# The first two w_in steps in four pieces each, and a room that the list now knows of

## The chip, the cores and the metric

The kernel runs on one core of a Trainium2 chip. The metric is the device time of one execution in microseconds; of the kernel before, three runs gave a median of 867.49 (867.4 to 868.03). Engines are named as in the profile: PE is TensorE (matmuls; PEld its weight loads), DVE is VectorE, ACT is ScalarE, POOL is GpSimd, SP is SyncE, which here issues DMAs.

## The reference

Attention inside chunks of 64 positions, and then a feed-forward layer whose nonlinearity is h·cos(h), all in fp32:

```python
scores = scale * np.matmul(q_c, k_c.transpose(0, 1, 2, 4, 3))
scores = scores - np.max(scores, axis=-1, keepdims=True)
attn = np.exp(scores)
attn = attn / (np.sum(attn, axis=-1, keepdims=True) + 1e-09)
out = np.matmul(attn, v_c)
...
x = np.ascontiguousarray(attn_out.transpose(0, 2, 1, 3)).reshape(B * S, H * D)
...
h = x @ w_in
g = h * np.cos(h)
return (g @ w_out).astype(np.float32)
```

q, k and v are (8, 8, 576, 64): 4608 tokens, 8 heads of 64. w_in is 512 x 2048, w_out 2048 x 512.

## The kernel before

**Tiles and steps.** The tokens are nine tiles of 512 (index t). The 512 columns of x are four groups of 128, one for each pair of heads (hp, or cc in the hidden layer); the 2048 hidden columns are 16 blocks of 128 (fc). A step is one tile with one block. `hidden` makes the block's h for the tile: each operand is split into a high and a low part, and each of the four groups of x takes three matmuls (high·high, high·low, low·high), twelve in all, which add up in one PSUM bank named h. There are two such banks. `activated` turns h into g = h·cos(h) in six pieces that alternate between ACT and DVE: a rounding (ACT, L497), the range reduction (DVE, L498), the sine (ACT, L499), the product with h (DVE, L500, the last reader of the bank h), g's high part (ACT, L501) and its low part (DVE, L502). `project` multiplies g by a block of w_out, twelve matmuls into the four banks acc, three steps behind `hidden` (LAG).

**Order of the steps.** Tile 0 with blocks 0 to 7 (steps 0 to 7), tile 1 with all 16 (steps 8 to 23), tile 0 with blocks 8 to 15 (steps 24 to 31), then tiles 2 to 8. While the first 32 steps run, the weights arrive over DMA and are split: a joining on DVE (L255, after two ACT pieces), a high part (ACT, L270) and a remainder (DVE, L275).

**Attention.** For tiles 0 and 1 `early` works by pairs of heads: scores on PE, a maximum (L333) and a subtraction (L337) on DVE, the exponential on ACT (L376), sums (L386) and a reciprocal on DVE, the quotient (L396, on POOL for tile 1 and for pairs 0 and 1 of tile 0, on DVE for the others), transposes on PE (L405), a copy on ACT (L411), and the weighted sum on PE. Then x goes into two parts: a cast on ACT (L460) and a remainder on DVE (L463). For tile 2 `attend_third` does the same for two groups of two pairs, with transposes on DVE (L422). The banks a0 and a1 carry the scores and the weighted sums of tiles 1 and 2, each in turn, so a later use waits for the last reader of the earlier one.

**x's room.** Tiles 0 and 1 have rooms of their own; tile 2's x is written into tile 1's (`x_room`). It can be written when step 23, the last of tile 1, has read what stood there.

**What sets the order.** Up to step 31 every piece of work on PE, ACT, DVE, POOL and SP is entered in a list with `piece(engine, length, run, *after, lag=...)`: its length in us as the list takes it, and the pieces that it comes after. `in_order` tries 1500 variations of due times, places each on the list's own clock (`placed`), keeps the best and gives the order in which all instructions are issued. Each engine then runs its instructions strictly in that order, and waits at the head of its queue for what the data need, whether the list knew of the need or not. The list before did not have an edge from step 23 to the casts of tile 2's x. From step 32 on a loop with an order written by hand takes over, which the change does not touch.

Of the kernel before, what the change touches and what calls it, by code (L numbers as in the profile page):

```python
# [11 lines left out]
F32 = mybir.dt.float32  # L12
# [9 lines left out]
P = 128  # L22
TOK = 512
# [8 lines left out]
GROUP = 8  # L32

EARLY = 2

PAIRED = 9

# [121 lines left out]
def attention_then_cos_ffn(ctx: ExitStack, tc, qT, kT, v, w_in, w_out, out, wide):  # L159
# [147 lines left out]
    def bank(kind, i):  # L307
        if kind == "a":
            b = ps_a.tile([P, 512], F32, name=f"a{i % 2}")
        else:  # L310
            b = ps_o.tile([P, 512], F32, name=f"acc{i}")
        return b
# [160 lines left out]

    partial = [hbm.tile([P, DM], F32, name=f"partial{sub}") for sub in range(NSUB)]

    def hidden(t, fc):
        h = ps_h.tile([P, TOK], F32, name="h")
        w_hi, w_lo = w_parts["in", fc]
        for cc in range(NCC):
            x_hi, x_lo = (x[:, cc % 2] for x in x_parts[t, cc // 2])  # L480
            ws = slice(cc * P, (cc + 1) * P)
            matmul(h, w_hi[:, ws], x_hi, start=(cc == 0), stop=False)
            matmul(h, w_hi[:, ws], x_lo, start=False, stop=False)
            matmul(h, w_lo[:, ws], x_hi, start=False, stop=(cc == NCC - 1))
        return h
# [119 lines left out]
    def piece(eng, length, run, *after, at=0.0, lag=0.15, port=False, table=None):  # L605
        port = port or eng == POOL
        work.append([eng, length, run, [a for a in after if a is not None], at, length + lag, port, table])
        return len(work) - 1
# [28 lines left out]
    def made_by(key, run, *args):  # L637

        def go():
            made[key] = run(*args)  # L640
        return go

    def rest_of(key, i):
        return lambda: made[key][i]()
# [26 lines left out]
    def early(t):  # L671
        s, e, z, q, w, p = {}, {}, {}, {}, {}, {}
        for hp in range(HP):
            which = ("a", hp % 2) if t else ("acc", hp)
            key = ("s", t, hp)
            s[hp] = piece(
                PE, 1.0, made_by(key, lambda hp=hp, which=which: scores_early(t, hp, bank(*which))),
                banks_free.get(("a", hp % 2)) if t else None,
                at=here["qk", t, hp], lag=0.35,
            )  # L680
            m = piece(DVE, 0.6, rest_of(key, 0), s[hp])
            room = turned_out.get((t - 1, hp // 2))
            banks_free[which] = piece(DVE, 0.6, rest_of(key, 1), m, room)
            e[hp] = piece(ACT, 0.6, lambda hp=hp: exponentials(t, hp), banks_free[which], table=AF.Exp)
# [9 lines left out]
        for hp in range(HP):  # L694
            key = ("t", t, hp)
            at = banks_free["a", hp % 2] if t else p.get(hp - 2)
            turned_out[t, hp // 2] = turned = piece(
                PE, 0.6, made_by(key, transposed, t, hp), q[hp], at, w.get(hp - 2), lag=0.35
            )
            p[hp] = piece(ACT, 0.5, lambda key=key: made[key](), turned, w.get(hp - 2))  # L700
            if t:
# [4 lines left out]
            if t and hp % 2 == 0:  # L706
# [3 lines left out]
            n = len(hps)  # L710
            key = ("x", t, hp)
            now = piece(
                PE, 0.9 * n, made_by(key, lambda hps=hps, which=which: weighted(t, hps, [bank(*b) for b in which])),
                *(p[j] for j in hps), *(banks_free.get(b) for b in which),
                at=here["v", 0, hp] if t == 0 else 0.0, lag=0.35,
            )
# [13 lines left out]
    ahead = early(1)  # L730


    def attend_third(begin):
        t = 2
        below = []
        for g in range(2):
# [16 lines left out]
        for g in range(2):  # L753
# [17 lines left out]
                        load_v(t, hp)  # L771
                piece(SP, 0.1, values_next, w)
            for i in (0, 2):
                hi = piece(ACT, 0.45, rest_of(key, i), w)
                banks_free["a", i // 2] = piece(DVE, 0.6, rest_of(key, i + 1), hi)
                x_done.setdefault(t, []).append(banks_free["a", i // 2])

# [17 lines left out]
    for s in range(STAGE):  # L795
        t, fc = order[s]
        key = ("h", s)
        bank_at = held.get(s - 2) if s > 1 else None
        stream = piece(
            PE, 2.72, made_by(key, hidden, t, fc), stream, split["in", fc], bank_at,  # L800
            *x_done[t], *([turned_out[0, 1]] if s < 2 else ()),
        )
        hid = stream
        if s == GROUP:
            def prefetch_third():
# [35 lines left out]
                held[s] = a  # L841
        given[s] = a
        if s == GROUP + 7:
            attend_third(hid)

    for i in in_order(work, x_done[2]):
        work[i][2]()
# [70 lines left out]
```

## Time and profile before

| what | us |
|---|---|
| median of three runs | 867.49 (867.4 to 868.03) |
| the profiled execution | 865.84 |
| its span, first to last instruction | 864.1 |

The profile is of one execution. A row of its timeline has a start, a duration, the engine, the line, the operation with its tiles, the count of instructions merged into it, and, in brackets, the idle time of the engine just before and what ended it. The rows that carry the argument stand in the prediction.

### The profile page before, as it was taken

The page shows a single profiled execution, that of the slowest core. Times are in us where ns is not written, and L with a number is a line of the kernel's source. Part 1 is how long each engine was busy: PE and PEld are TensorE (multiplying, and loading weights), DVE is VectorE, ACT ScalarE, POOL GpSimd, SP SyncE. Part 2 cuts the span into 40 slices and gives each one's busy share as a digit, 9 for nine tenths or more (in the row PEclk, how much of TensorE's full clock was granted, in tenths as well). Part 3 has the DMA queues.
Part 4 walks back from the last instruction along what each step waited for, and adds up shares of the span by engine and source line. Part 5 has one row for each costly group of instructions (what it writes and reads, how often), then busy time and mean ns, then how long its engine had stood idle before and what let it go on. Part 6 is the DMA issues. An engine that isn't in the chain of part 4 may idle for free.

```text
span 864.1 us, 14053 instructions
## 1 busy us (share of the span) xinstructions
PE 845.4 (98%) x5792; PEld 695.1 (80%) x5792; DVE 555.0 (64%) x942; ACT 389.5 (45%) x636; POOL 7.5 (1%) x12
## 2 busy tenths in 40 slices
PE   6999999799999999999999999999999999999998
PEld 5778888688888888888888888888888888888886
DVE  6979878644686567665776468645865577644332
ACT  5999963333433335333533353334433353333332
POOL 1020000000000000000000000000000000000000
PEclk9999999999999999999999999999999999999999
DMA  9990200320103000300130010301030010001001
GB/s 344 416 376 34 75 2 26 120 99 2 50 1 122 25 13 37 123 25 2 49 110 15 25 49 15 109 25 50 1 122 25 2 50 25 1 1 49 1 1 49
DMA packets 26559, 57.52 MB, mean 67 GB/s; under 512 B 2944, under 2 KB 2944, under 8 KB 26496
## 3 DMA queue, kind: packets, MB, share of 16 engines
q1 hardware_dynamic: 26496, 56.63, 18.1%
q8 instruction: 45, 0.74, 0.4%
q14 instruction: 18, 0.15, 0.0%
HBM read 46.14 MB, written 10.49 MB: 66 GB/s over the span
## 4 chain that ended last, share of the span: by engine, by line
PE 92%; DVE 1%; issue 0%; ACT 0%
PE acc L193 45%; PE h L193 43%; PE a L193 4%; DVE pts L422 1%; DVE x L463 0%; DVE g L498 0%; PE a L405 0%; DVE x L561 0%; ACT x L460 0%; DVE g L500 0%
## 5 line engine op out<-in xcount | busy, mean ns | idle before, releaser
L193 PE MATMUL h<-x,w_in 128*128 128x512 f32 x1728 | 417.2, 390 | 4.8 <-DVE g L500 4.8
L193 PEld LDWEIGHTS h<-x,w_in 128*128 128x128 f32 x1728 | 324.9, 188 | 72.8 <-DVE g L500 5.3
L193 PE MATMUL acc<-w_out,g_hi 128*128 128x512 f32 x1152 | 358.4, 392 | 0.0
L193 PEld LDWEIGHTS acc<-w_out,g_hi 128*128 128x128 f32 x1152 | 214.0, 188 | 45.5 <-ACT pts L559 0.3
L193 PE MATMUL acc<-w_out,g_lo 128*128 128x512 f32 x576 | 224.4, 390 | 0.0
L498 DVE SCALAR_TENSOR_TENSOR g<-g,h 128x512 f32<-128x512 int32 x144 | 98.6, 685 | 143.4 <-ACT g L497 142.5
L497 ACT ACTIVATE g<-h 128x512 int32<-128x512 f32 x144 | 85.8, 596 | 195.2 <-PE h L193 194.8
L502 DVE TENSOR_TENSOR g_lo<-g,g_hi 128x512 fp32r<-128x512 f32 x144 | 99.6, 691 | 75.3 <-ACT g_hi L501 73.1
L499 ACT ACTIVATE g<-g 128x512 f32<-128x512 f32 x144 | 91.2, 633 | 124.5 <-DVE g L498 124.4
L501 ACT CAST g_hi<-g 128x512 fp32r<-128x512 f32 x144 | 89.4, 621 | 124.6 <-DVE g L500 78.2
L500 DVE TENSOR_TENSOR g<-h,g 128x512 f32<-128x512 f32 x144 | 99.5, 691 | 53.7 <-ACT g L499 50.6
L193 PEld LDWEIGHTS acc<-w_out,g_lo 128*128 128x128 f32 x576 | 108.1, 188 | 22.8
L422 DVE STREAM_TRANSPOSE pts<-e 32x256 f32<-32x256 f32 x224 | 97.4, 435 | 3.7
L463 DVE TENSOR_TENSOR x<-a,x 128x512 fp32r<-128x512 f32 (+1 forms) x36 | 22.3, 654 | 7.7 <-ACT x L460 7.7
L386 DVE TENSOR_REDUCE z<-e 128x8 f32<-128x512 f32 x36 | 23.7, 678 | 3.2 <-ACT e L376 3.2
L255 DVE SCALAR_TENSOR_TENSOR w<-w,half 128x512 uint32<-128x512 uint32 x32 | 22.6, 713 | 2.8 <-ACT half L262 1.6
L193 PEld LDWEIGHTS a<-kt,qt 64*64 64x64 f32 x1024 | 18.3, 135 | 7.4 <-issue 5.6
L376 ACT ACTIVATE e<-e 128x1024 f32<-128x1024 f32 (+1 forms) x22 | 19.1, 900 | 9.2 <-DVE e L337 9.1
L193 PE MATMUL a<-kt,qt 64*64 64x64 f32 x1024 | 20.6, 221 | 1.6 <-DVE x L463 1.6
L193 PEld LDWEIGHTS a<-pts,vt 64*64 64x64 f32 x1056 | 17.3, 137 | 6.0 <-issue 4.6
L460 ACT CAST x<-a 128x512 fp32r<-128x512 f32 (+1 forms) x36 | 18.5, 565 | 7.7 <-PE h L193 7.2
L396 DVE TENSOR_TENSOR e<-e,z 128x512 f32<-128x512 f32 x30 | 20.3, 683 | 0.0
(50 smaller groups left out, 252.2 us busy)
## 6 DMA issues: line engine op xcount, KB each, us to landing
qt<-in_qT_dram SPq DMA_DIRECT2D x36, 256.0 KB, 4.9
kt<-in_kT_dram SPq DMA_DIRECT2D x36, 256.0 KB, 5.1
vt<-in_v_dram SPq DMA_DIRECT2D x34, 256.0 KB, 3.7
w_in<-in_w_in_dram SPq DMA_DIRECT2D x16, 512.0 KB, 9.7
w_out<-in_w_out_dram SPq DMA_DIRECT2D x16, 512.0 KB, 9.9
out_dram<-w SPq DMA_DIRECT2D x16, 256.0 KB, 2.2
out_dram<-half SPq DMA_DIRECT2D x16, 256.0 KB, 2.1
out_dram<-x SPq DMA_DIRECT2D x4, 256.0 KB, 2.0
```

The costliest lines, as they stand in the source:

```text
L193: kept(nc.tensor.matmul(*args, **kw))
L255: kept(nc.vector.scalar_tensor_tensor(bits, bits, 3, low, op0=ALU.logical_shift_left, op1=ALU.bitwise_or))
L386: kept(nc.vector.tensor_reduce(out=sums_of(t)[:, hp], in_=weights_of(t, hp // 2)[:, hp % 2], op=ALU.add, axis=AX.X))
L396: kept(eng.tensor_tensor(e, e, zb, op=ALU.mult))
L422: kept(nc.vector.transpose(out=dst[o : o + BL, :, qb], in_=src[i : i + BL, :, kb]))
L463: kept(nc.vector.tensor_tensor(lo, xq, hi.bitcast(F32), op=ALU.subtract))
L497: lambda: kept(nc.scalar.activation(n, h, AF.Identity, bias=0.25, scale=0.5 / math.pi)),
L498: lambda: kept(nc.vector.scalar_tensor_tensor(g, n, -2.0 * math.pi, h, op0=turns, op1=over)),
L499: lambda: kept(nc.scalar.activation(g, g, AF.Sin, bias=0.5 * math.pi)),
L500: lambda: kept(nc.vector.tensor_tensor(g, h, g, op=ALU.mult)),
L501: lambda: kept(nc.scalar.copy(out=g_hi, in_=g)),
L502: lambda: kept(nc.vector.tensor_tensor(g_lo, g, g_hi.bitcast(F32), op=ALU.subtract)),
```

## The change

The edits:

- `hidden` can do a part of the four groups of x, and go on in a bank that it began.
- Steps 0 and 1 (`s < APART`) enter the list as four pieces of three matmuls each, one per pair of heads. Each comes after its own pair's x only, where a whole block came after all four.
- The casts of tile 2's x come after `room`, which is the hidden block of step 23. For this the list gets `attend_third` eight steps later in the program text (at `GROUP + NFC - 1`), with the same `begin`.
- Three lengths in the list are shorter: scores 0.95 for 1.0, transposes 0.53 for 0.6, weighted sums 0.55 a pair for 0.9.
- No matmul, no DMA and no piece of ACT or DVE work is added or taken away, except that tables for ACT's functions are loaded where the order asks for them.

```diff
-    def hidden(t, fc):
-        h = ps_h.tile([P, TOK], F32, name="h")
+    def hidden(t, fc, ccs=range(NCC), h=None):
+        if h is None:
+            h = ps_h.tile([P, TOK], F32, name="h")
         w_hi, w_lo = w_parts["in", fc]
-        for cc in range(NCC):
+        for cc in ccs:
...
-                PE, 1.0, made_by(key, lambda hp=hp, which=which: scores_early(t, hp, bank(*which))),
+                PE, 0.95, made_by(key, lambda hp=hp, which=which: scores_early(t, hp, bank(*which))),
...
-                hi = piece(ACT, 0.45, rest_of(key, i), w)
+                hi = piece(ACT, 0.45, rest_of(key, i), w, room)
...
-        stream = piece(
-            PE, 2.72, made_by(key, hidden, t, fc), stream, split["in", fc], bank_at,
-            *x_done[t], *([turned_out[0, 1]] if s < 2 else ()),
-        )
+        if s < APART:
+            for cc in range(NCC):
+                run = lambda key=key, t=t, fc=fc, cc=cc: made.update(
+                    {key: hidden(t, fc, (cc,), made.get(key))})
+                stream = piece(
+                    PE, 0.68, run, stream, split["in", fc], bank_at, turned_out[0, 1],
+                    *x_done[t][2 * cc : 2 * cc + 2], lag=0.15 if cc == NCC - 1 else 0.0,
+                )
+        else:
+            stream = piece(
+                PE, 2.72, made_by(key, hidden, t, fc), stream, split["in", fc], bank_at, *x_done[t],
+            )
...
-            attend_third(hid)
+            begin = hid
+        if s == GROUP + NFC - 1:
+            attend_third(begin, hid)
```

The list makes a new order of all that comes before step 32. The lines of the kernel move with the diff: L193 becomes L195, L460 L462, L463 L465, L497 L501, L498 L502, L499 L503, L500 L504. The order below step 32 is the same.

On PE, at the first hidden step. Before, the last weighted sum of tile 0 (a1_407, a0_406) is followed by two score groups of tile 1 (a0_438, a1_458), and then step 0 (h_479) with x of pairs 0 and 1 (x0_333, x0_334) and of pairs 2 and 3 (x0_400, x0_401):

```order
L193 MATMUL a1_407<-pts_372,x1_148 64x64 x2
L193 MATMUL a0_438<-kt_153,qt_152 64x64 x16
L193 MATMUL a1_458<-kt_157,qt_156 64x64 x16
L193 MATMUL h_479<-x0_333,w_in0_357 128x512
L193 MATMUL h_479<-x0_334,w_in0_357 128x512
...
L193 MATMUL h_479<-x0_400,w_in0_357 128x512
L193 MATMUL h_479<-x0_401,w_in0_357 128x512
```

and now, where step 0 is h_428, pairs 0 and 1 are x0_334 and x0_335, and pairs 2 and 3 x0_403 and x0_404:

```order
L195 MATMUL acc3_409<-pts_372,x1_148 64x64 x2
L195 MATMUL h_428<-x0_334,w_in0_369 128x512
L195 MATMUL h_428<-x0_335,w_in0_369 128x512
...
L195 MATMUL a1_442<-kt_157,qt_156 64x64 x16
L195 MATMUL a0_465<-kt_153,qt_152 64x64 x16
L195 MATMUL h_428<-x0_403,w_in0_369 128x512
L195 MATMUL h_428<-x0_404,w_in0_369 128x512
```

The first six matmuls of step 0 moved ahead of the two score groups; the other six stand behind them. Step 1 is cut in the same way around the third score group, where it stood whole between the third and the fourth. On DVE, ahead of this, the second pair's sum and the first reciprocal of tile 0 moved behind the third pair's subtraction and the fourth pair's maximum, and the join of w_in 0 moved behind the quotients of pairs 2 and 3.

On ACT, where tile 2's first x is cast. Before, h_1679, h_1757 and h_1804 are steps 21, 22 and 23, and x1_1753 is the high part of x:

```order
L499 ACTIVATE g_1710<-g_1710 128x512
L501 CAST g_hi_1711<-g_1710 128x512
L460 CAST x1_1753<-a0_1719 128x8x64
L460 CAST x1_1753<-a1_1720 128x8x64
L497 ACTIVATE g_1795<-h_1757 128x512
L497 ACTIVATE g_1834<-h_1804 128x512
L499 ACTIVATE g_1795<-g_1795 128x512
L499 ACTIVATE g_1834<-g_1834 128x512
```

and now, with h_1756 and h_1802 for steps 22 and 23:

```order
L503 ACTIVATE g_1710<-g_1710 128x512
L505 CAST g_hi_1711<-g_1710 128x512
L501 ACTIVATE g_1793<-h_1756 128x512
L503 ACTIVATE g_1793<-g_1793 128x512
L505 CAST g_hi_1794<-g_1793 128x512
L501 ACTIVATE g_1834<-h_1802 128x512
L462 CAST x1_1753<-a1_1720 128x8x64
L462 CAST x1_1753<-a0_1719 128x8x64
L503 ACTIVATE g_1834<-g_1834 128x512
```

Both casts moved behind all of step 22 and the first piece of step 23. On DVE the remainders that belong to them moved likewise, and on PE the second weighted sum of tile 2 moved from ahead of a projection to behind it.

On ACT again, some 25 instructions after the first sine: before, g_696 is step 4, and e0 and e1 are the exponentials of tile 1:

```order
L497 ACTIVATE g_696<-h_658 128x512
L260 ACTIVATE w_701<-w_out3_98 128x512
L376 ACT_TABLE_LOAD
L376 ACTIVATE e0_455<-e0_455 128x512
L499 ACT_TABLE_LOAD
L499 ACTIVATE g_696<-g_696 128x512
L376 ACT_TABLE_LOAD
L376 ACTIVATE e1_521<-e1_521 128x512
```

and now, with g_722 for step 4:

```order
L378 ACT_TABLE_LOAD
L378 ACTIVATE e0_459<-e0_459 128x512
...
L378 ACTIVATE e1_531<-e1_531 128x512
L262 ACTIVATE w_719<-w_out3_98 128x512
L501 ACTIVATE g_722<-h_654 128x512
L378 ACTIVATE e1_531<-e1_531 128x512
L272 CAST w_in6_741<-w_691 128x512
L503 ACT_TABLE_LOAD
L503 ACTIVATE g_722<-g_722 128x512
```

The sine of step 4 moved behind all three exponentials that were spread over three loads of their table; between the first sine and the last of these exponentials there were four table loads after the first sine's, and now there are two.

More of the change, by code (lines that the diff above doesn't have):

```diff
@@ L34 @@
 EARLY = 2
+APART = 2
 PAIRED = 9
@@ L697, in early @@
             turned_out[t, hp // 2] = turned = piece(
-                PE, 0.6, made_by(key, transposed, t, hp), q[hp], at, w.get(hp - 2), lag=0.35
+                PE, 0.53, made_by(key, transposed, t, hp), q[hp], at, w.get(hp - 2), lag=0.35
             )
@@ L712, in early @@
             now = piece(
-                PE, 0.9 * n, made_by(key, lambda hps=hps, which=which: weighted(t, hps, [bank(*b) for b in which])),
+                PE, 0.55 * n, made_by(key, lambda hps=hps, which=which: weighted(t, hps, [bank(*b) for b in which])),
                 *(p[j] for j in hps), *(banks_free.get(b) for b in which),
@@ L730, in attention_then_cos_ffn, with attend_third @@
     ahead = early(1)
-    def attend_third(begin):
+    def attend_third(begin, room):
         t = 2
```

## The prediction

> **What bounds the kernel now.** I read the page's first and fourth parts, then the busy times stretch by stretch, then TensorE's own waits.
>
> ```profile
> span 864.1 us, 14053 instructions
> PE 845.4 (98%) x5792; PEld 695.1 (80%) x5792; DVE 555.0 (64%) x942; ACT 389.5 (45%) x636; POOL 7.5 (1%) x12
> PE 92%; DVE 1%; issue 0%; ACT 0%
> ```
>
> TensorE (PE) is busy for 845.4 of 864.1 us and holds 92% of the chain that ended last. The change removes no matmul, so it can only win idle TensorE time and the time in which TensorE runs below full clock. The busy times by stretch (PE, PEld, DVE, ACT, POOL, granted clock, DMA) say where those lie:
>
> ```profile
> 0.00:25.00 25.00, 15.39 (x337) 13.75 (x337) 16.45 (x33) 13.49 (x27) 2.74 (x8) 0.93 0.95 353
> 25.00:60.00 35.00, 35.00 (x269) 28.28 (x268) 29.76 (x50) 33.92 (x56) 4.77 (x4) 1.00 1.01 408
> 60.00:100.00 40.00, 39.34 (x235) 32.20 (x235) 35.42 (x58) 39.52 (x75) 0.00 (x0) 1.00 0.28 95
> 100.00:140.00 40.00, 40.00 (x294) 32.86 (x293) 34.96 (x60) 25.82 (x42) 0.00 (x0) 1.00 0.00 1
> 140.00:180.00 40.00, 35.16 (x265) 28.33 (x265) 24.89 (x46) 12.62 (x22) 0.00 (x0) 0.96 0.24 79
> 330.00:864.00 534.00, 530.50 (x3388) 436.37 (x3386) 324.17 (x551) 203.91 (x325) 0.00 (x0) 1.00 0.11 37
> ```
>
> Idle are 9.61 us before 25, 0.66 between 60 and 100, 4.84 between 140 and 180, and 3.50 in the last stretch (the program's end, which the change does not touch). ACT, 45% busy over the span, is full from 25 to 100: 33.92 of 35 and 39.52 of 40. There a delay on ACT finds little slack to hide in.
>
> **Term A, the third tile's x.** TensorE around the 4.84 (start, duration, instruction), and below it the same kinds of work undisturbed:
>
> ```profile
> 157.02 0.61 PE L193 MATMUL acc<-w_out,g_hi 128*128 128x512 f32 x2
> 164.74 4.44 PE L193 MATMUL h<-x,w_in 128*128 128x512 f32 x12 [4.84 <-DVE g L500]
> 169.11 1.16 PE L193 MATMUL a<-pts,vt 64*64 64x64 f32 x64
> 170.20 0.74 PE L193 MATMUL acc<-w_out,g_hi 128*128 128x512 f32 x2
> ...
> 106.81 2.88 PE L193 MATMUL h<-x,w_in 128*128 128x512 f32 x12
> 109.62 1.16 PE L193 MATMUL a<-kt,qt 64*64 64x64 f32 x64
> 110.71 0.73 PE L193 MATMUL acc<-w_out,g_hi 128*128 128x512 f32 x2
> 113.56 2.88 PE L193 MATMUL h<-x,w_in 128*128 128x512 f32 x12
> ```
>
> The hidden block of step 24 waits for DVE's L500, which frees the bank of step 22. ACT and DVE show why that came late:
>
> ```profile
> 154.30 2.88 PE L193 MATMUL h<-x,w_in 128*128 128x512 f32 x12
> 155.63 1.08 ACT L460 CAST x<-a 128x512 fp32r<-128x512 f32 x2 [7.15 <-PE h L193]
> 156.59 1.23 ACT L497 ACTIVATE g<-h 128x512 int32<-128x512 f32 x2
> 158.59 3.13 DVE L422 STREAM_TRANSPOSE pts<-e 32x256 f32<-32x256 f32 x7
> 161.75 0.69 DVE L498 SCALAR_TENSOR_TENSOR g<-g,h 128x512 f32<-128x512 int32 x1
> 164.00 0.68 DVE L500 TENSOR_TENSOR g<-h,g 128x512 f32<-128x512 f32 x1
> ```
>
> The two casts of tile 2's x stand idle at ACT's head for 7.15 us, until step 23 (from 154.30) has read the first half of tile 1's x, whose room they overwrite. Step 22's first activation stands behind them, and on DVE its L498 stands behind the x remainders and seven transposes. In the changed order ACT runs step 22's three pieces and step 23's first one before these casts, and DVE has step 22's L498 ahead of the remainders. Then step 22 goes as an undisturbed step does: its matmuls end near 151.6, the activation takes about 0.6, L498 0.69, the sine about 0.6 and L500 0.69, so the bank is free near 154.5. Step 24 wants it at 157.02 + 2.72 = 159.7: 5.2 us of slack. What is late next is the second weighted sum, which needs both banks from the remainders. These now follow step 23's activation: casts to 158.9, remainders and transposes to about 162.9 (four or five DVE pieces of 0.44 to 0.69). TensorE reaches it only after step 24 and one projection, at 159.7 + 2.8 + 2.7 = 165.2. So 2.3 us remain.
>
> Price: from the projection at 157.02 to the one at 170.20 pass 13.18. Undisturbed the pieces are a projection (106.81 to 113.56 is block, scores and projection: 2.81 + 1.09 + 2.85), so 2.72 + 2.81 + 1.09 = 6.62. **A = -6.56**: 4.84 of waiting and the rest because the block itself took 4.44 where 2.88 is usual. The granted clock shows this:
>
> ```profile
> 164.00:165.00 1.00, 0.26 (x1) 0.26 (x2) 0.97 (x3) 0.88 (x2) 0.00 (x0) 0.70 0.00 0
> 165.00:166.00 1.00, 1.00 (x3) 0.81 (x4) 0.97 (x3) 0.37 (x2) 0.00 (x0) 0.50 0.00 0
> ```
>
> The clock goes to 0.50 after the wait, and comes back within the block. Bounds of A: -6.6, all of it, and -4.8, if the slow stretch should come anyway.
>
> **Term B, the first hidden steps.** TensorE and the pieces that lead to it:
>
> ```profile
> 11.15 0.67 DVE L386 TENSOR_REDUCE z<-e 128x8 f32<-128x512 f32 x1
> 12.48 2.04 POOL L396 TENSOR_TENSOR e<-e,z 128x512 f32<-128x512 f32 x2 [11.18 <-DVE z L391]
> 16.51 1.29 DVE L396 TENSOR_TENSOR e<-e,z 128x512 f32<-128x512 f32 x2
> 21.00 0.34 PE L193 MATMUL a<-pts,x 64*64 64x64 f32 x7
> 22.45 0.75 DVE L463 TENSOR_TENSOR x<-a,x 128x256 fp32r<-128x256 f32 x2
> 22.92 2.08 PE L193 MATMUL a<-kt,qt 64*64 64x64 f32 x64 [1.59 <-DVE x L463]
> 24.93 3.03 PE L193 MATMUL h<-x,w_in 128*128 128x512 f32 x12
> 27.89 1.15 PE L193 MATMUL a<-kt,qt 64*64 64x64 f32 x32
> ```
>
> Before, TensorE stands 1.59 us for the last remainder of tile 0's x, then does two score groups (2.01) and only then block 0 (2.96). After, six matmuls of block 0 come first. They need the x of pairs 0 and 1, not of 2 and 3. The price of the new DVE order: a subtraction and a maximum of the later pairs move ahead of the second sum (11.15). At 0.6 each, and with a short wait for the third pair's scores, POOL's quotients start 1.2 to 1.4 later, and so do the first transposes. The later pairs' work no longer stands behind that, so their quotients (16.51) end 0.2 to 0.3 earlier. From there to the last remainder DVE does eight remainders and two weight remainders as before, and two joins in place of one (0.6 more): the last remainder ends 0.2 to 0.4 later, at about 23.5 for 23.2. TensorE ended the weighted sums at 21.34 (21.00 + 0.34); I put that at 21.9, half of POOL's delay, since the later pairs' quotients come earlier. By then DVE's order has the first x and w_in 0 complete (near 21.4). So half of block 0, 1.4 us, runs from 21.9 to 23.3, in the hole; the two score groups end at 25.3 for 24.93, and block 0 at 26.8 for 27.89: **B = -1.1**. The other cuts (four pieces per block, block 1 around a score group) add no matmul, and accumulate in one bank as before. Bounds: -1.9, the whole idle time between 19.32 and 22.92 (3.60 less 1.71 busy), and +1.4, if POOL's delay went through in full:
>
> ```profile
> 19.32:22.92 3.60, 1.71 (x64) 1.33 (x65) 3.53 (x9) 3.09 (x9) 0.00 (x0) 1.00 1.03 416
> ```
>
> **Term C, ACT between 25 and 62.** ACT is full here, so it decides whether B reaches the end.
>
> ```profile
> 47.33 1.28 ACT L499 ACT_TABLE_LOAD   x1
> 48.62 0.63 ACT L499 ACTIVATE g<-g 128x512 f32<-128x512 f32 x1
> 49.28 0.69 DVE L500 TENSOR_TENSOR g<-h,g 128x512 f32<-128x512 f32 x1 [0.17 <-ACT g L499]
> 52.98 3.00 PE L193 MATMUL h<-x,w_in 128*128 128x512 f32 x12
> 59.65 0.39 PE L193 MATMUL acc<-w_out,g_lo 128*128 128x512 f32 x1
> 60.69 1.22 PE L405 MATMUL a<-ident,e 128*128 128x128 f32 x8 [0.66 <-DVE x L463]
> ```
>
> Before, step 4's bank is free at 49.97, and step 6 takes it at 52.98: 3 us of slack. After, step 4's sine stands behind three exponentials in a row. Counted along ACT's queue from about 22.6 at 0.5 to 0.57 an instruction and 1.28 a table load, that sine starts near 50.3 and L500 ends at 51.7. TensorE, 1.1 early, wants the bank at 51.9. With half a us of doubt in the count that is nothing to 0.7 us of new wait; I take +0.4. In return ACT's order has three table loads up to there where it had five (2.56 less), so the casts of the next x come about 2 us earlier, and the wait at 60.69 (due at 59.65 + 0.23, so 0.81) goes: -0.8. **C = -0.4**, bounds -0.8 and +1.8 (ACT late by another 2.2, with the old wait back in part). Behind 62 weights and quotients are several us ahead of their use, and from 100 on ACT has 14 us free in 40.
>
> The Trainium skill (ScalarE: Activation LUTs, What ACT_TABLE_LOAD costs) gives a switch of tables as 1283 ns and a drain of about 1380 ns. Here the sine begins 1.29 after its load began, and the load 0.03 after the exponential before it ended, so no drain shows; with it, two loads ahead of step 4's sine would add 2.8 and make the sum -5.3. The trace speaks against that, and I keep 1.28.
>
> **Sum.** -6.56 - 1.1 - 0.4 = -8.1. The profiled execution took 865.84 (span 864.1 and 1.7 around it): 857.7. The runs' median, 867.49, lies 1.65 above that execution, so 867.49 - 8.1 = **859.4**.
>
> **Rivals.**
> - *B is lost on ACT.* A comes, but weights or casts arrive later than I count, step 6 waits 1 to 3 us, and B and C come out at nothing to +1.5. For it: ACT is full, and POOL's delay is certain. Against: two table loads fewer. 861 to 862.5.
> - *A low clock falls on the first blocks.* TensorE now idles from about 11.5 to 15.0 in place of the 2.06 before 13.57, and after the long wait at 160 the clock was 0.50 for some three us. If that falls on 21 to 25, where matmuls are dense, it costs up to half of 3.4, so 1.7: 861.1. Before 25 the mean clock was 0.93 already, so one slow stretch is paid for in either kernel. The Trainium skill (TensorE: Matmul & The Clock Gate, Part 1: The HAM clock gate) says that an idle window of about 3.4 us halves the clock, and that the window runs freely, so its place changes from run to run. The 0.50 agrees; the place no run here shows.
> - *A's wait moves* to the second weighted sum, should the remainders come later than 165.2; each us beyond costs one. With 2 to 5 us of it, 861.5 to 865.
> - *Slower than before.* The place is step 4's sine on ACT's queue. TensorE follows it one for one once step 4's bank is late, because step 6 stands first in its queue and everything behind it. It gives back C and B at 1.5 us beyond my count, and A too at about 8: then the time passes 867.5, say 870. ACT would have to lose 8 us between 22 and 50, of which the trace shows no sign: it ran there with 1.08 of 35 us idle.
> - *The change doesn't do it.* The list might have put the casts ahead again; the order of ACT excludes that.
>
> **How the numbers follow.** Forecast 0.72 (858 to 861), B lost 0.11, low clock 0.06, moved wait 0.05, something slower than before 0.02, the rest (0.04) for B at its better bound. The range has the forecast, B lost and the low clock: 857.5 to 862.5; what is left out is the moved wait, the slower case and the tails of the forecast's own terms. 0.2%, 1.7 us, is about what a measurement of this kernel can tell from no change. Faster by more than that is every case but the slower one, less 0.05 for a wait that I have not seen: 0.93; within 0.04; slower 0.03.
>
> **What would show it.** Right: between 140 and 180 TensorE idles under 0.3 and the clock stays 1.00; the casts L462 wait behind step 23's activation; blocks of step 0 begin near 22 and scores stand between their halves; step 6 near 51.9. Wrong: a wait of TensorE on DVE's L504 before step 6 above 1 us; one on L465 before the second weighted sum; a clock of 0.50 after 20.

## The result, and the profile after

| kernel | median us | all runs | ratio to before |
|---|---|---|---|
| before | 867.61 | 867.4 to 868.03 (4 runs) | 1 |
| changed | 859.59 | 858.82 to 860.8 (4 runs) | 0.9908 [0.9891, 0.9925] |

The profiled execution of the changed kernel was the slowest of its four (860.8, span 859.0), while that of before was below all its other runs (865.84, span 864.1). So the two profiles lie 5.1 us apart and the medians 8.0. The page of after:

```profile
span 859.0 us, 14061 instructions
PE 844.9 (98%) x5792; PEld 695.1 (81%) x5792; DVE 555.2 (65%) x942; ACT 387.1 (45%) x634; POOL 7.1 (1%) x12
```

Of the work that counts as busy, two table loads fewer are all that changed in number (ACT 634 for 636). The busy times by stretch, with the columns as before (PE, PEld, DVE, ACT, POOL, granted clock, DMA):

```profile
0.00:25.00 25.00, 15.28 (x277) 13.37 (x278) 14.69 (x29) 11.85 (x24) 2.75 (x8) 0.86 0.95 351
25.00:60.00 35.00, 34.36 (x320) 27.81 (x319) 30.92 (x53) 32.44 (x56) 4.32 (x4) 1.00 0.98 396
60.00:100.00 40.00, 39.84 (x239) 32.76 (x238) 36.26 (x59) 39.78 (x75) 0.00 (x0) 1.00 0.31 106
140.00:180.00 40.00, 40.00 (x295) 32.80 (x294) 28.96 (x54) 15.87 (x27) 0.00 (x0) 1.00 0.24 83
```

Between 140 and 180 TensorE now does 295 matmuls without an idle moment and at full clock, where it did 265. Between 60 and 100 the idle time is 0.16 for 0.66. But up to 25 it did 277 matmuls where it had done 337, at a clock of 0.86 for 0.93, and between 25 and 60 stand 0.64 us idle that were not there.

Three marks on TensorE take the difference apart: the start of step 2's block (the first of a merged row of blocks), the start of step 23's, and the end of the span. The timeline of after around the second mark, TensorE first, then ACT:

```profile
155.51 2.88 PE L195 MATMUL h<-x,w_in 128*128 128x512 f32 x12
...
160.95 2.88 PE L195 MATMUL h<-x,w_in 128*128 128x512 f32 x12
...
166.48 1.16 PE L195 MATMUL a<-pts,vt 64*64 64x64 f32 x64
158.49 0.60 ACT L501 ACTIVATE g<-h 128x512 int32<-128x512 f32 x1 [1.78 <-PE h L195]
158.98 1.07 ACT L462 CAST x<-a 128x512 fp32r<-128x512 f32 x2
```

The casts run behind step 23's activation, step 24 follows (160.95) without a wait, and so does the second weighted sum (166.48). Before, these marks were 33.00, 154.30 and 864.1; now they are 34.87 (below), 155.51 and 859.0. The first of them, before:

```profile
33.00 5.75 PE L193 MATMUL h<-x,w_in 128*128 128x512 f32 x24
```

| stretch | before | after | difference | predicted |
|---|---|---|---|---|
| start to step 2 (B) | 33.00 | 34.87 | +1.87 | -1.1 |
| step 2 to step 23 (C) | 121.30 | 120.64 | -0.66 | -0.4 |
| step 23 to the end (A) | 709.80 | 703.49 | -6.31 | -6.56 |

The wait before the transposes behind step 4's projection, 0.66 before, is 0.16, and step 6 takes its bank without a wait (TensorE):

```profile
55.05 2.99 PE L195 MATMUL h<-x,w_in 128*128 128x512 f32 x12
...
62.68 0.63 PE L407 MATMUL a<-ident,e 128*128 128x128 f32 x4 [0.16 <-DVE x L465]
```

A came as forecast, and C somewhat larger than forecast. B did not come at all, in this execution. The same timeline at the start:

```profile
15.87 2.12 PE L407 MATMUL h<-ident,e 128*128 128x128 f32 x8 [3.69 <-POOL e L398]
...
22.67 0.69 PE L195 MATMUL a<-pts,x 64*64 64x64 f32 x32 [0.67 <-DVE x L465]
23.15 0.68 PE L195 MATMUL acc<-pts,x 64*64 64x64 f32 x32
23.76 1.66 PE L195 MATMUL h<-x,w_in 128*128 128x512 f32 x6
25.35 2.08 PE L195 MATMUL a<-kt,qt 64*64 64x64 f32 x64
27.36 0.73 PE L195 MATMUL h<-x,w_in 128*128 128x512 f32 x2
28.73 2.45 PE L195 MATMUL h<-x,w_in 128*128 128x512 f32 x10 [0.64 <-issue]
...
34.87 1.42 PE L195 MATMUL h<-x,w_in 128*128 128x512 f32 x5
```

The first half of block 0 stands in front of the two score groups, as the change wants it, but starts at 23.76, not 21.9. And its second half stops after two matmuls and goes on at 28.73: 0.64 us idle that the profile puts down to "issue", a wait for nothing that it shows. That wait was in no part of the prediction.

### The profile page after: what moved, and what is told of

It is laid out like the page before. It is cut to its first block, busy times and chain, and to the rows that moved or that the text cites. A ratio compares the mean times of both kernels' runs of the same rounds, so it can differ in the third digit from the quotient of the medians.

```text
span 859.0 us, 14061 instructions
## 1 busy us (share of the span) xinstructions
PE 844.9 (98%) x5792; PEld 695.1 (81%) x5792; DVE 555.2 (65%) x942; ACT 387.1 (45%) x634; POOL 7.1 (1%) x12
## 4 chain that ended last, share of the span: by engine, by line
PE 93%; DMA 5%; ACT 1%; DVE 1%; SPq 0%; issue 0%; POOL 0%; ACTq 0%
PE acc L195 46%; PE h L195 43%; PE a L195 4%; DMA w_in<-in_w_in_dram 3%; DMA vt<-in_v_dram 1%; DMA kt<-in_kT_dram 1%; PE h L407 0%; DVE g_lo L506 0%; DVE x L465 0%; ACT e L378 0%; SPq L192 0%; ACT w L262 0%; POOL e L398 0%; ACT g_hi L505 0%; ACT pts L413 0%
## 5 line engine op out<-in xcount | busy, mean ns | idle before, releaser
L195 PE MATMUL h<-x,w_in 128*128 128x512 f32 x1728 | 416.2, 390 | 0.6 <-issue 0.6
L195 PEld LDWEIGHTS h<-x,w_in 128*128 128x128 f32 x1728 | 323.8, 188 | 68.2 <-issue 0.8
L195 PE MATMUL acc<-w_out,g_hi 128*128 128x512 f32 x1152 | 358.0, 392 | 0.0
L195 PEld LDWEIGHTS acc<-w_out,g_hi 128*128 128x128 f32 x1152 | 214.1, 188 | 45.1
L195 PE MATMUL acc<-w_out,g_lo 128*128 128x512 f32 x576 | 224.4, 390 | 0.0
L502 DVE SCALAR_TENSOR_TENSOR g<-g,h 128x512 f32<-128x512 int32 x144 | 98.7, 685 | 141.5 <-ACT g L501 140.5
L501 ACT ACTIVATE g<-h 128x512 int32<-128x512 f32 x144 | 86.0, 597 | 196.3 <-PE h L195 195.2
L503 ACT ACTIVATE g<-g 128x512 f32<-128x512 f32 x144 | 91.1, 633 | 122.8 <-DVE g L502 122.7
L504 DVE TENSOR_TENSOR g<-h,g 128x512 f32<-128x512 f32 x144 | 99.5, 691 | 55.2 <-ACT g L503 52.1
L195 PEld LDWEIGHTS acc<-w_out,g_lo 128*128 128x128 f32 x576 | 108.1, 188 | 22.8
L378 ACT ACTIVATE e<-e 128x1024 f32<-128x1024 f32 (+1 forms) x22 | 19.0, 897 | 10.3 <-DVE e L339 10.2
L465 DVE TENSOR_TENSOR x<-a,x 128x512 fp32r<-128x512 f32 (+1 forms) x36 | 22.3, 655 | 1.9 <-ACT x L462 1.7
L195 PEld LDWEIGHTS a<-kt,qt 64*64 64x64 f32 x1024 | 18.3, 135 | 6.0 <-issue 5.6
L195 PEld LDWEIGHTS a<-pts,vt 64*64 64x64 f32 x1056 | 17.5, 137 | 6.1 <-issue 4.6
L195 PE MATMUL a<-kt,qt 64*64 64x64 f32 x1024 | 20.6, 221 | 0.0
L398 DVE TENSOR_TENSOR e<-e,z 128x512 f32<-128x512 f32 x30 | 20.4, 684 | 0.0
L195 PE MATMUL a<-pts,vt 64*64 64x64 f32 x1056 | 20.0, 224 | 0.0
```

The source lines that it names most:

```text
L195: kept(nc.tensor.matmul(*args, **kw))
L398: kept(eng.tensor_tensor(e, e, zb, op=ALU.mult))
L465: kept(nc.vector.tensor_tensor(lo, xq, hi.bitcast(F32), op=ALU.subtract))
L501: lambda: kept(nc.scalar.activation(n, h, AF.Identity, bias=0.25, scale=0.5 / math.pi)),
L502: lambda: kept(nc.vector.scalar_tensor_tensor(g, n, -2.0 * math.pi, h, op0=turns, op1=over)),
L503: lambda: kept(nc.scalar.activation(g, g, AF.Sin, bias=0.5 * math.pi)),
```

## The experiments

The order of work up to step 31 is a list of 594 pieces. The experiments run the changed kernel's pieces in an order written out by hand, `AFTER` being the list of the changed kernel and `BEFORE` that of the kernel before in the same pieces. Both lists hold the same pieces in three parts: up to 80 (the end of step 0), from 80 to 483, and from 483 (the casts of tile 2's x) on. A kernel is then one line:

```diff
-    for i in in_order(work, x_done[2]):
+    for i in BEFORE[:80] + AFTER[80:]:
         work[i][2]()
```

The lists stand ahead of the functions, so lines move: the changed kernel's L195 is L251 or L225 below, L407 is L463 or L442, L398 L454, L465 L521, L504 L560. The first four kernels ran on one chip, where before had a median of 867.36.

**The third tile's part alone**: `BEFORE[:483] + AFTER[483:]`.

> The order of before up to the casts of tile 2's x, and from there the order of the changed kernel; the first steps uncut. My theory (the casts at ACT's head cost 4.84 us of waiting and 1.6 of half clock): 6.6 us faster than before, near 861.0, TensorE without idle time between 140 and 180 and the clock 1.00 there. Rival (the slow stretch comes anyway, and only the wait goes): 4.8 faster, near 862.8, with a clock of 0.50 somewhere after 150.

861.37 us, 0.9932 [0.9917, 0.9947]. By the ratio A alone is worth 5.9 us, 4.6 to 7.2. By the marks it is 6.2: from step 23 (156.04) to the end of the span (859.6) are 703.56, before 709.80. The rest was lost at the start, which is the old one here: the granted clock was 0.50 from about 23.6 to 27.0, on two score groups and block 0, and step 2 began at 34.74, where before has 33.00:

```profile
23.18 3.34 PE L251 MATMUL a<-kt,qt 64*64 64x64 f32 x64 [1.59 <-DVE x L521]
26.46 3.25 PE L251 MATMUL h<-x,w_in 128*128 128x512 f32 x12
...
34.74 5.74 PE L251 MATMUL h<-x,w_in 128*128 128x512 f32 x24
```

```profile
25.00:26.00 1.00, 1.00 (x25) 1.00 (x22) 1.00 (x2) 0.80 (x3) 0.00 (x0) 0.50 1.05 408
```

**All but the third tile's part**: `AFTER[:483] + BEFORE[483:]`.

> The order of the changed kernel up to the casts of tile 2's x, and from there that of before. The prediction's terms B and C: 1.5 us faster than before, near 866.1, with the wait of 4.8 back. Rival (read from the changed kernel's profile, where step 2 begins at 34.87 for 33.00 and step 7 at 63.07 for 61.67): the start loses, 1.4 slower than before, near 869.0.

867.8 us, 1.0005 [0.9996, 1.0015]. Start and middle together gain nothing that can be measured; the forecast was -1.5. The wait is back in TensorE's timeline:

```profile
155.84 2.88 PE L251 MATMUL h<-x,w_in 128*128 128x512 f32 x12
...
166.28 5.33 PE L251 MATMUL h<-x,w_in 128*128 128x512 f32 x12 [4.84 <-DVE g L560]
```

From 155.84 to the end of its span, 866.5, are 710.66, for 703.49 in the changed kernel: A measured by its removal is 7.2. The same 4.84 of waiting costs 7.2 here and 6.3 in the execution of before, because the block behind it took 5.33 here and 4.44 there.

**The start undone**: `BEFORE[:80] + AFTER[80:]`.

> The order of before up to the end of step 0 (block 0 whole, behind two score groups), then the order of the changed kernel. By the prediction's B (the cut start wins 1.1): 1.1 slower than the changed kernel, near 860.7. Rival (POOL's quotients 1.6 later and a second slow stretch make the cut start lose): up to 1.9 faster than the changed kernel, 857.7 to 859, with the first transposes about 1.5 earlier in its profile than the changed kernel's.

859.14 us, 0.9912 [0.9897, 0.9927]. The changed kernel has 0.9908. With the start of before the kernel is as fast: by its time B is nothing that can be measured. Step 2 begins at 33.25 in its profile.

**Half a block ahead, and nothing else of the start**: `BEFORE[:54] + [259, 260] + BEFORE[54:71] + BEFORE[73:80] + AFTER[80:]`, where 259 and 260 are the first six matmuls of block 0, and 54 is the place ahead of the two score groups. DVE, ACT and POOL keep the start of before.

> As old_start, but the first six matmuls of block 0 stand ahead of the two score groups, with the order of before kept on DVE, ACT and POOL. If a half block fits into the 1.59 us hole before the scores, as the prediction's B says of the idea: 1.4 faster than old_start. Rival (what comes behind is bound by ACT and DVE up to step 6, so that TensorE waits there instead): within 0.4 of old_start.

857.97 us, 0.9896 [0.9880, 0.9913]: the lowest of these four, though its interval overlaps that of the kernel with the start undone. TensorE's timeline:

```profile
13.68 0.66 PE L463 MATMUL h<-ident,e 128*128 128x128 f32 x4 [2.41 <-POOL e L454]
...
21.03 1.64 PE L251 MATMUL h<-x,w_in 128*128 128x512 f32 x6
22.70 2.08 PE L251 MATMUL a<-kt,qt 64*64 64x64 f32 x64
24.71 3.02 PE L251 MATMUL h<-x,w_in 128*128 128x512 f32 x12
...
31.38 4.88 PE L251 MATMUL h<-x,w_in 128*128 128x512 f32 x20
```

So the idea of B works in this execution: half a block fits into the hole, and step 2 begins at 31.38 for 33.00. There is no wait on issue in it. What the changed kernel adds to it in the start (DVE's, ACT's and POOL's new order, other transposes first) brought no further gain.

The next four ran together (before: 867.57).

**The middle undone**: `AFTER[:80] + BEFORE[80:483] + AFTER[483:]`.

> The first 80 pieces (up to the end of step 0) and the third tile's part stand as in the changed kernel, the pieces between them as in the kernel before: term C is undone alone. Theory P (C = -0.4, as predicted): 859.6 + 0.4 = 860.0. Theory M (the middle is worth what lies between the two earlier kernels with the old start, 861.4 - 859.1 = 2.2): 861.6 to 861.8, with the wait of 0.7 to 0.8 on the joined weights' side near 61 back and more table loads on ACT. Theory N (those 2.2 were spread between runs only): 859.0 to 860.0.

860.94 us, 0.9928 [0.9915, 0.9940]. The changed kernel's order has 0.9908, and 0.9917 further below: by these ratios the middle would be worth 1.0 to 1.7, which lies between theories P and M. TensorE's waits have the old one back in full:

```profile
PE a L463 <- DVE x L521: 0.7, 1, 0.7
```

From step 2 (33.33) to step 23 (154.66) its profile has 121.33, before 121.30, the changed kernel 120.64. So the marks give C as -0.7, without the noise of the start.

**The middle alone**: `BEFORE[:80] + AFTER[80:483] + BEFORE[483:]`.

> Only the pieces after step 0 and ahead of the third tile's part stand as in the changed kernel; start and third tile as before. Theory P: 867.4 - 0.4 = 867.0. Theory M (the middle is worth 2.2 by itself): 865.2. Theory S (what the middle wins is swallowed by the old wait of 4.8 us near 160, which does not depend on it): 867.4, with that wait longer than 4.84 by what was won.

866.34 us, 0.9991 [0.9982, 0.9999]: by the ratio -0.8 (-1.6 to -0.1). Theory M (865.2) is out, P stands, and by its marks (33.21 to 153.88, 120.67 for 121.30) C is -0.6. The wait near 160 is 4.84 again, so theory S falls too: it follows TensorE and swallows nothing.

**TensorE kept at work in the idle stretch**: the changed kernel's order, and 14 calls (28 matmul instructions) ahead of the first transposes.

```diff
+        if "warm" not in made:
+            made["warm"] = True
+            spare = bank("a", 0)
+            for c in range(WARM):
+                matmul(spare[:, c % 4 * P : (c % 4 + 1) * P], ident, ident, start=True, stop=True)
         pt = ps_h.tile([P, 512], F32, name="h") if t == 0 else bank("a", hp)
```

> The changed kernel with 14 matmuls more, identity by identity into a bank that nothing reads, ahead of the first transposes, where TensorE idled 3.7 us. Theory L (the two stretches at half clock from 15 to 21.7 are what took B's gain): clock 1.00 through 25, the first half of block 0 about 0.5 to 1.5 earlier relative to the first transposes, time 858.1 to 859.1. Theory Q (the lateness is POOL's quotients and the chain over ACT and DVE, and the clock costs nothing on it): clock higher, time 859.3 to 860.0. Slower, 860.5 or more, if the added matmuls end after POOL's quotients.

858.39 us, 0.9904 [0.9887, 0.9922]. No stretch of low clock is left up to 25 in its profile. TensorE:

```profile
12.38 3.53 PE L225 MATMUL a<-ident 128*128 128x128 f32 x28
15.75 0.60 PE L442 MATMUL h<-ident,e 128*128 128x128 f32 x4
...
22.13 1.64 PE L225 MATMUL h<-x,w_in 128*128 128x512 f32 x6
...
25.71 3.05 PE L225 MATMUL h<-x,w_in 128*128 128x512 f32 x12
...
32.42 3.94 PE L225 MATMUL h<-x,w_in 128*128 128x512 f32 x16
```

From the first transposes to half block 0 pass 6.38, in the changed kernel's profile 7.89. Step 2 begins at 32.42 for 34.87, and the time lies where theory L put it. But the second half of block 0 also has no wait on issue any more. Two things changed at once, so this run does not show that the clock alone took B's gain; and its interval overlaps the changed kernel's.

**The same in the kernel with half a block ahead** (10 calls).

> The kernel with six matmuls of block 0 ahead of the two score groups and DVE, ACT and POOL as before in the start, with 10 matmuls more, identity by identity into a bank that nothing reads, in the idle stretch of 2.4 us ahead of the first transposes. Theory L: no stretch at half clock between 15 and 19, half block 0 at 20 to 20.5 in place of 21.0, time 857.0 to 857.6. Theory Q: 857.8 to 858.2, the weighted sums wait on ACT and DVE instead.

857.88 us, 0.9894 [0.9879, 0.9908]. The clock is 1.00 all along, and half block 0 starts at 21.34, no earlier than the 21.03 without: as theory Q has it, there the low clock falls on transposes and weighted sums with waits for DVE and ACT between them (0.74 and 0.67 us in this profile), so that a higher clock gains nothing that shows.

The last four again share a chip (before: 867.28).

**The changed kernel's order, written out**: `AFTER`.

> The order of the changed kernel, written out as a list of numbers: no other difference. 859.6, single runs between 858.5 and 861. It stands beside the other three for a comparison on one chip.

860.38 us (858.99 to 861.06), 0.9917 [0.9902, 0.9932]. The order is that of the changed kernel, and yet the start of this execution is another one, on POOL and on TensorE:

```profile
13.18 2.04 POOL L454 TENSOR_TENSOR e<-e,z 128x512 f32<-128x512 f32 x2 [11.87 <-ACT half L320]
14.28 0.66 PE L463 MATMUL h<-ident,e 128*128 128x128 f32 x4 [3.98 <-POOL e L454]
...
21.81 1.64 PE L251 MATMUL h<-x,w_in 128*128 128x512 f32 x6
...
25.39 0.74 PE L251 MATMUL h<-x,w_in 128*128 128x512 f32 x2
26.96 2.46 PE L251 MATMUL h<-x,w_in 128*128 128x512 f32 x10 [0.83 <-issue]
...
33.08 3.27 PE L251 MATMUL h<-x,w_in 128*128 128x512 f32 x13
```

The transposes come 1.6 us earlier than in the first profile of this order, since POOL does. Its TensorE had ended the scores of tile 0 at 10.29, there at 12.18: the queries and keys arrived earlier. Half block 0 starts at 21.81, where the prediction has 21.9. The wait on issue is at the same instruction.

**POOL's delay taken away**: the changed kernel with the first 21 pieces in the order of before, `BEFORE[:17] + [182, 173, 171, 181] + [i for i in AFTER if i not in BEFORE[:21]]`. Pieces 181 and 182 are POOL's quotients, in the changed kernel's order.

> The changed kernel, with DVE's first eleven pieces and the ACT pieces among them in the order of before: the second sum and the reciprocal of the first two pairs stand ahead of the third pair's subtraction again, and POOL starts its quotients earlier. Theory D (POOL's delay is what took B): POOL begins near 12.6 in place of 14.8, first transposes near 14.0, half of block 0 near 22.0, time 858.0 to 858.6. Theory I (the order of the transposes and the wait put down to issue took it): 859.2 to 860.0 although POOL is earlier.

859.79 us, 0.9912 [0.9897, 0.9926]. POOL begins at 13.04, 1.6 after the end of tile 0's scores, where the changed kernel's two profiles have 2.6 and 2.9 and those with the old start 0.7 to 1.5. Half block 0 starts at 22.26 and the wait on issue is 0.83. The time lies where theory I put it, not theory D, and the wait on issue is there although POOL is earlier. How much POOL's delay cost the run does not tell, because the clock is 0.50 from 13.3 to 20.1 here, twice as long as in the written-out order's profile.

**TensorE's program moved on by 28 matmuls**: the changed kernel's order, and the 14 calls at the very start, while TensorE waits for the first keys. With their weight loads these are 56 instructions (14117 in the span for 14061).

```diff
+        if "shift" not in made:
+            made["shift"] = True
+            spare = bank("a", 0)
+            for c in range(SHIFT):
+                matmul(spare[:, c % 4 * P : (c % 4 + 1) * P], ident, ident, start=True, stop=True)
         for c in range(NCH):
```

> The changed kernel with 14 identity matmuls more at the very start, while TensorE waits for the first queries and keys: every later instruction of TensorE stands 28 places further on, the idle stretch of 3.7 us near 13 stays. Theory F (the wait of 0.6 to 1.1 us put down to issue in the second half of block 0 hangs on the instruction's place in the program): that wait is gone or has moved, time 858.8 to 859.2. Theory G (it hangs on what happens around it in time): the wait is there as before, at the third matmul of that half, time 859.6. In either, low clock from about 15 on as in the changed kernel.

872.07 us, 1.0055 [1.0043, 1.0068], which no theory expected. Theory F's sign is there all the same. The idle stretch (4.32) and the stretch of low clock behind it are there, and the wait on issue is gone:

```profile
14.97 2.12 PE L442 MATMUL h<-ident,e 128*128 128x128 f32 x8 [4.32 <-POOL e L433]
...
22.05 1.66 PE L225 MATMUL h<-x,w_in 128*128 128x512 f32 x6
...
25.66 3.05 PE L225 MATMUL h<-x,w_in 128*128 128x512 f32 x12
...
32.38 3.98 PE L225 MATMUL h<-x,w_in 128*128 128x512 f32 x16
```

From half block 0 to step 2 are 10.33, in the first profile of the changed kernel 11.11 and in the second 11.27. The time itself says nothing on the start, since all later matmuls are slower (last section).

**Half a block ahead, once more**, beside the changed kernel's order on one chip.

> The same kernel as the one with six matmuls of block 0 ahead of the two score groups and the start's other engines as before, once more beside the changed kernel on one chip. If its lead is real: 857.6 to 858.4, 1.2 to 2 less than the changed kernel. If it came from a lucky place of the clock's window: 859 to 859.6.

859.03 us, 0.9900 [0.9882, 0.9919], for 860.38: 1.35 less. Its median is lower again, by as much as a real lead was to give, but the intervals overlap, and its own time lies where the lucky place of the clock's window was to put it. So the two theories are not told apart. Its times were 1.1 higher than in the first go, and this profile shows one reason:

```profile
25.28 0.72 PE L251 MATMUL h<-x,w_in 128*128 128x512 f32 x2
26.85 2.44 PE L251 MATMUL h<-x,w_in 128*128 128x512 f32 x10 [0.85 <-issue]
...
32.94 3.27 PE L251 MATMUL h<-x,w_in 128*128 128x512 f32 x13
```

Here the wait on issue is there, at the same instruction as in the changed kernel; in the first profile of the same kernel it was not.

**All the starts side by side.** Each row is one profile; the last column is the stretch at a granted clock of 0.50, worked out from windows of one microsecond.

| kernel | first transposes | first half of block 0 | wait on issue | step 2 | half block to step 2 | clock 0.50 |
|---|---|---|---|---|---|---|
| before | 13.58 | block whole | none | 33.00 | | 14.2 to 17.6 |
| start undone | 13.92 | block whole | none | 33.25 | | 15.1 to 18.5 |
| middle alone | 13.83 | block whole | none | 33.21 | | 14.2 to 17.6 |
| third tile alone | 13.83 | block whole | none | 34.74 | | 13.4 to 20.2, 23.6 to 27.0 |
| changed | 15.87 | 23.76 | 0.64 | 34.87 | 11.11 | 14.8 to 21.7 |
| changed, written out | 14.28 | 21.81 | 0.83 | 33.08 | 11.27 | 15.2 to 18.6 |
| middle undone | 14.57 | 22.03 | 0.83 | 33.33 | 11.30 | 15.4 to 18.8 |
| third tile undone | 15.74 | 23.63 | 1.12 | 35.16 | 11.53 | 14.3 to 21.1 |
| POOL's delay away | 14.14 | 22.26 | 0.83 | 33.55 | 11.29 | 13.3 to 20.1 |
| half block ahead, 2nd | 13.92 | 21.60 | 0.85 | 32.94 | 11.34 | 14.1 to 17.5 |
| half block ahead, 1st | 13.68 | 21.03 | none | 31.38 | 10.35 | 15.3 to 18.7 |
| half block ahead, kept at work | 13.99 | 21.34 | none | 31.69 | 10.35 | none |
| changed, kept at work | 15.75 | 22.13 | none | 32.42 | 10.29 | none |
| changed, program moved on | 14.97 | 22.05 | none | 32.38 | 10.33 | 14.9 to 18.3 |

The column "half block to step 2" falls into two groups: 10.3 where there is no wait on issue, 11.1 to 11.5 where there is one. In the four profiles with the old start there is none.

**What the wait on issue waits for.** A trace also keeps the DMA packets with their queue and kind. The changed kernel and the one whose program was moved on have on their pages:

```profile
q8 instruction: 45, 0.74, 0.3%
```

```profile
q8 instruction: 46, 0.75, 0.3%
```

These packets have 16384 bytes each. Against them stand 11684 instructions on TensorE in the first trace and 11740 in the second, about 256 a packet; the engine with the next most has about a tenth of that. So the queue carries TensorE's program, as far as sizes and counts tell. The second of its packets lands close to the interruption:

| profile | packet ended | third matmul of the second half | between | wait on issue |
|---|---|---|---|---|
| changed | 27.25 | 28.73 | 1.48 | 0.64 |
| changed, written out | 25.70 | 26.96 | 1.26 | 0.83 |
| middle undone | 25.76 | 27.21 | 1.45 | 0.83 |
| third tile undone | 27.60 | 29.05 | 1.45 | 1.12 |
| POOL's delay away | 26.13 | 27.44 | 1.31 | 0.83 |
| half block ahead, 2nd | 25.44 | 26.85 | 1.41 | 0.85 |
| half block ahead, 1st | 23.74 | 25.28 | 1.54 | none |

In the three profiles with matmuls added ahead of block 0, which have no wait either, the packet had ended by 23.0. So the wait fits a packet of TensorE's instructions that comes late: TensorE goes on 1.3 to 1.5 us after its end, and in the profiles where it ended earlier than that there is no wait. The packet records do not say which instructions they hold, so this is inferred and not shown outright.

## Why the prediction was right, and where it was not

The time was forecast as 859.4 and came as 859.59; the second measurement of the same order lies 0.8 higher. A, four fifths of the sum, was right in size and in mechanism. That the sum came out within 0.2 us is luck: B was lost, C was 0.3 larger, A may have been up to 0.6 larger, and the rest is the spread between executions.

- **Term A held.** Predicted -6.56 (bounds -6.6 to -4.8). The marks show -6.3 against before's profile and -7.2 against the kernel with only this part undone; alone it measured -5.9 by the ratio (-4.6 to -7.2) and -6.2 by the marks. The mechanism is as told: casts behind step 23's activation, no idle time between 140 and 180, clock 1.00, and no wait at the second weighted sum, so the rival of a moved wait is out. The bound of -6.6 was too tight: how long the block behind the wait runs at half clock is not fixed (it took 4.44, 4.62 and 5.33 in three profiles with the same 4.84 of waiting).
- **Term C held.** Predicted -0.4, from a new wait of +0.4 before step 6 and an old one of -0.8. By the marks it is -0.66, and -0.6 to -0.7 in the other profiles with the new middle and no matmuls added. The old wait went from 0.66 idle to 0.16, and before step 6 no new one shows. Step 6 begins 20.18 after step 2, before 19.98, so the new delay is 0.2 at most. The count along ACT's queue had step 4's sine near 50.3; it ran at 53.59, but TensorE came to step 6 as much later (55.05 for 51.9), so the bank was free just in time. The saving of table loads is as the prediction counts it, five up to this wait and now three; the three exponentials of before stood behind two loads of their own table (45.38 and 49.27), not three. The "slower" rival, and the one of B lost on ACT, are out: it was not ACT that took B.
- **Term B failed**, -1.1 predicted. Three pairs of kernels differ in the start alone: the changed kernel and the one with the start undone (859.59 and 859.14 us, ratios 0.9908 and 0.9912), the middle undone and the third tile's part alone (0.9928 and 0.9932), and the third tile undone and the middle alone (1.0005 and 0.9991). The new start is 0.3 better, 0.3 better and 1.2 worse; in the second pair the kernel with the old start had the low clock on its first blocks, so that 0.3 is no gain of the new start. Without low clock there the old start has step 2 at 33.00 to 33.25, the changed kernel's order at 33.08 and 34.87. Its steps one by one:
  - *"So half of block 0, 1.4 us, runs from 21.9 to 23.3, in the hole"*: right where the scores of tile 0 come early (21.81, 22.03), late by 1.9 where they come late (23.76). Whether half of POOL's delay was the right share stays open: the delay itself was forecast as 1.2 to 1.4 and was 2.29 in the first profile (12.48 to 14.77), 0.66 of it because tile 0's scores ended later (12.18 for 11.52), and with most of it undone the half block started at 22.26, under a longer low clock.
  - *"the two score groups end at 25.3 for 24.93, and block 0 at 26.8 for 27.89"*: this failed. In the written-out profile the half block began at 21.81, as forecast, but block 0 ended near 27.9 (its last four matmuls are the first of the ten at 26.96, some 0.24 each), where it had ended before, because its second half was interrupted after two matmuls. *"The other cuts add no matmul, and accumulate in one bank as before"* held no price for that. All five profiles with the changed start and TensorE's instructions at their own places have the interruption; it costs 0.8 to 1.2 (11.1 to 11.5, less 10.3), as much as B was to bring. It goes when TensorE's program is moved on by 28 matmuls, with the low clock still there. The place in the program alone does not decide it, since one program had the wait in one profile and not in the other; together with the packets above this points to instructions that had not arrived, though the profile names no releaser.
- **The low clock rival** (0.06) holds in part. The clock was 0.50 until 21.7 in the changed kernel's profile, which the prediction named as a sign against itself. It fell on transposes and weighted sums there, not on the first blocks. With it the way from the first transposes to half block 0 took 7.9 us, 7.5 in the written-out profile with its shorter stretch, and 6.4 with TensorE kept at work. On the first blocks it fell in another kernel, the third tile's part alone, and cost there about what the rival had put (1.7): step 2 at 34.74 for 33.00. The single runs point the same way. In the written-out order the run with a mean granted clock of 0.998 took 858.99, the three with 0.996 took 860.21 to 861.06; with the start undone it was 858.78 to 859.19 at 0.998 and 860.86 at 0.996. So part of the spread between runs goes with low clock. The Trainium skill (TensorE: Matmul & The Clock Gate, Part 1: The HAM clock gate) says that the window runs freely, so that its place changes from run to run. The prediction said that no run showed the place; the two profiles of the changed order, 14.8 to 21.7 and 15.2 to 18.6, agree with it, though their idle stretches did not begin at the same time either.

What is left of B is the version with half a block ahead and the old start on the other engines: 857.97 and 859.03 us, the first 1.6 below the changed kernel's first measurement, the second 1.35 below the changed order on the same chip. With 10 more matmul calls in its idle stretch it took 857.88, no clear gain. Both beat the kernel before and, by medians, the changed one; single runs of the two overlap, and so do the intervals of half a block ahead and of the start undone (857.97 and 859.14 on one chip).

Why the second packet started at 22.67 in the first profile of half a block ahead and at 24.39 in the second, with the same instructions at the same places, stays open. So does which part of the changed start other than the interruption keeps it behind half a block ahead: its half block starts 0.2 to 2.7 later than there, and the runs do not tell the order of the transposes from that of DVE's remainders.

## What to carry to other kernels

Split a trace at a few fixed marks on the engine that bounds it, and compare stretch by stretch: the sum here was right to a fifth of a microsecond, by luck, and only the marks show that one term of it was lost. Where a kernel's start depends on arriving data, take two or three profiles of it before pricing an edit of a microsecond there, because the same order began step 2 at 33.08 and at 34.87. A long matmul group that is cut, with many short matmuls between its parts, is not free merely because it adds no instruction; look for idle time put down to issue, and for packets of the kind "instruction" that end shortly before TensorE goes on.

## What the runs showed of the hardware that was not expected

The wait on issue: TensorE stands 0.6 to 1.1 us in the middle of a matmul group, with weight loads idle as well, after 64 score matmuls of 64 by 64. It always comes after the second matmul of the second half, and not in every execution: of two profiles of half a block ahead one has it. In all six profiles that have it a packet of 16384 bytes on the instruction queue ended 1.3 to 1.5 us before TensorE went on.

Half clock after a short wait: in the profile of the third tile's part alone the clock fell to 0.50 at 23.6, after a wait of 1.59 us that ended at 23.18, while the wait after which the prediction saw it was 4.84.

The slow program: the 28 matmuls at the very start made the wide matmuls slower to the end, in each of five runs (871.74 to 873.14). The groups by form, first of the changed kernel, then of the one whose program was moved on (count, busy time, mean ns):

```profile
L195 PE MATMUL h<-x,w_in 128*128 128x512 f32 x1728 | 416.2, 390 | 0.6 <-issue 0.6
L195 PE MATMUL acc<-w_out,g_hi 128*128 128x512 f32 x1152 | 358.0, 392 | 0.0
```

```profile
L225 PE MATMUL h<-x,w_in 128*128 128x512 f32 x1728 | 424.9, 394 | 0.0
L225 PE MATMUL acc<-w_out,g_hi 128*128 128x512 f32 x1152 | 362.4, 396 | 0.0
L225 PE MATMUL a<-ident 128*128 128x128 f32 x28 | 5.0, 356 | 1.4 <-POOL ident masks.py:199 1.4
```

These two groups take 8.7 and 4.4 us more, 13.1 together. The median lies 13.7 above that of the kernel with the same 28 matmuls later, in the idle stretch (858.39), so it is their place and not their number. The granted clock reads 1.00 in both. Why work at the very start should slow all that follows by 1 to 2%, no run here tells.
